# A fused attention and two feed-forward layers: maxima of a block of v moved to a later unit, and eight stores of decoded weights spread over twenty units

## Chip, cores and metric

One core of one Trainium2 chip. The metric is the device time of one execution in microseconds (us), the median of several runs. Before the change three runs gave a median of 1037.03 us (1035.72 to 1040.48).

## What is computed

```python
def _attn_ref(q, k, v, tau):                      # q, k, v: 1 x 6016 x 256
    qn = q / (np.linalg.norm(q, axis=1, keepdims=True) + 1e-06)
    kn = k / (np.linalg.norm(k, axis=1, keepdims=True) + 1e-06)
    s = kn.transpose(0, 2, 1) @ qn / tau          # 256 x 256
    a = softmax of s over its last axis
    return v @ a
def _moe_ref(x, w_in, w_out):                     # 256 -> 2048 -> 256
    h = x @ w_in
    return (h * np.cos(h)) @ w_out
def _moe2_ref(x, w_in, w_out):                    # 256 -> 2048 -> 256
    h = x @ w_in
    return (h / (1.0 + np.exp(-h))) @ w_out
reference = moe2(moe(attn(q, k, v, tau)))
```

The weights arrive as 64-bit words and are decoded to float32 on the chip. Each matrix is held as a high and a low part, so that a product is three matmul passes (high-high, low-high, high-low).

## The kernel before

The 6016 tokens are cut into eleven blocks of 512 and one of 384 (`BLOCKS`, numbered 0 to 11). First the scores are summed over all tokens, and the softmax is folded into the first layer's weights `wa`. Then the first layer with its cosine runs over the blocks, and after it the second layer with its sigmoid. The change lies in the loop of the first layer (from L997).

A *unit* `(b, m)` is one block times one eighth of the 2048 hidden columns (m = 0 to 7). Sixteen units alternate between blocks 0 and 1 (`TURNS = 16`, loop index `i` below 16), then units follow block by block: i = 16 is (2, 0), i = 24 is (3, 0), and so on to block 11. There is no scheduler: `tc.manual_schedule()` takes the instructions of each engine in the order in which the loop emits them, and each engine and each DMA queue works its own list in that order. Unit i emits, in this order:

- on TensorE (PE) the products `h` (`emit_h`, L715, 12 matmuls); for the first unit of the next block, the `bound` (below) is also emitted in unit m = 7;
- on ScalarE (ACT) the cosine of `h` (`emit_first`, L726) and then the high part `hi` of the unit before (`emit_split`, L746); on VectorE (DVE) the low part `lo` of the unit before (L747), then the product with the cosine, `t` (`emit_cos`, L739);
- the eight stores of `wa` and `wo1` (L1027 to L1029, 1 MB each, two in each of the units i = 16 to 19) into the DRAM tiles `kept`, which only a fallback for large arguments (`general`) reads;
- from block 3 on, in units m = 0 and m = 5, one step of decoding the second layer's weights: ACT takes the absolute value (L315), POOL rounds the low word (L290), DVE clamps, shifts and joins the sign (L296, L297, L303), POOL adds the low word (L306) and builds the forms (L351, L353, L354), and the SyncE queue (SP) stores them (L967, L972) and loads the next raw 0.5 MB (L270);
- in unit m = 2 the load of the next block of v, `vraw` (L389, 0.5 MB, one buffer);
- in unit m = 3 the split of `vraw` on GpSimd (POOL: `xhi` L435, `xlo` L442), and `span_of`, the maxima over groups of 128 tokens of the absolute values of `vraw`, on DVE (L395);
- on PE the second product `o` of unit i - 2 (`emit_o1`, L757, 12 matmuls), which needs that unit's `hi` and `lo`;
- one step of preparing the previous block for the second layer (`emit_x2`): from m = 2 on `forms_first` (L767, DVE), `forms_second` (L772 and L773, DVE), the high parts (L778, ACT), the low parts (L786, DVE, in m = 5 and m = 6), and then the stores of `xs` (L831, SP).

`bound` (L419 to L429) multiplies the block's maxima by the weights' maxima (L423, PE) and keeps on DVE whether the cosine's argument is small (`small`, L427 to L429). It is emitted in unit m = 7 of the block before, and from block 2 on the cosine takes it as a factor. The first call of `span_of`, for block 2, stands in unit i = 14 (L1046).

Of the kernel before, what the change touches and what calls it, by code (L numbers as in the profile page):

```python
# [9 lines left out]
F32 = mybir.dt.float32  # L10
# [21 lines left out]
NB = len(BLOCKS)  # L32
# [34 lines left out]
TURNS = 16  # L67
# [153 lines left out]
def direct(ctx, tc, qk, vT, tau, w_in1, w_out1, w_in2, w_out2, outT, dp, kept, within):  # L221
    nc = tc.nc
# [14 lines left out]
    wa = [wp.tile(QUAD, F32R, tag="quad", name=f"wa{i}", bufs=8) for i in range(4)]  # L237
    wo1 = [wp.tile(QUAD, F32R, tag="quad", name=f"wo1_{i}", bufs=8) for i in range(4)]
# [117 lines left out]
    def w_in(w, name, to=None, size=PIECE, **kw):  # L356
        n = size // CH
        src = w.rearrange("(a p) f -> p a f", p=P)
        cut = [slice(j * n, (j + 1) * n) for j in range(DFF // n)]
        to = None if to is None else [to[:, :, c] for c in cut]  # L360
        return Weights(name, [src[:, :, c] for c in cut], to=to, size=size, **kw)

    def w_out(w, name, size=PIECE, **kw):
        n = size // C
        src = w.rearrange("(f p) e -> p f e", p=P)
        return Weights(name, [src[:, n * j : n * (j + 1), :] for j in range(NF // n)], size=size, **kw)
# [7 lines left out]
    def halves(t):  # L374
        return t.rearrange("p s (h b) -> p s h b", h=2)

    def turns(t):
        return t.rearrange("p s (b h) -> p s h b", h=2)
# [3 lines left out]
    def x_tile(s, b):  # L382
        t = xp.tile([P, NU, HB], F32R, tag=f"x{s}", name=f"x{s}{b}")
        return t.rearrange("p s c -> p (s c)")[:, : CH * TB].rearrange("p (a n) -> p a n", a=CH)
# [7 lines left out]
    def span_of(b, raw):  # L392
        t0, n = BLOCKS[b]
        m = most[b] = wp.tile([P, CH, TB // P], BF16, tag="most", name=f"most{b}", bufs=2)
        nc.vector.tensor_reduce(  # L395
            out=m[:, :, : n // P],
            in_=raw[:, :, :n].rearrange("p a (j n) -> p a j n", n=P),
            axis=AX.X,
            op=ALU.max,
            apply_absolute_value=True,  # L400
        )
# [29 lines left out]
    def split_v(b, raw, pool=False):  # L431
        n = BLOCKS[b][1]
        hi, lo = xparts[1, b] = [x_tile(s, b) for s in ("hi", "lo")]
        if pool:
            nc.gpsimd.tensor_scalar(  # L435
                out=halves(hi[:, :, :n]), in0=turns(raw[:, :, :n]), scalar1=1.0, scalar2=1.0, op0=ALU.mult, op1=ALU.mult
            )
        else:
            nc.scalar.activation(halves(hi[:, :, :n]), turns(raw[:, :, :n]), AF.Copy)

        def low():
            (nc.gpsimd if pool else nc.vector).tensor_tensor(  # L442
                out=halves(lo[:, :, :n]), in0=turns(raw[:, :, :n]), in1=halves(hi[:, :, :n]).bitcast(F32), op=ALU.subtract
            )

        return low
# [57 lines left out]
    def steps_of(names):  # L504
        for name in names.split():
            calls[name]()
# [36 lines left out]
    for g, n in enumerate(GROUPS):  # L543
# [22 lines left out]
        if g in FINE:  # L566
            k = len(fine)
# [46 lines left out]
    for a in range(CH):  # L614
        nc.vector.scalar_tensor_tensor(
            out=E[:, a], in0=S[a], scalar=r[:, 1, a : a + 1], in1=rq, op0=ALU.mult, op1=ALU.mult
# [88 lines left out]
    def h_room(u):  # L705
        return next_room().tile([P, 2, TB], F32, tag="h", name=f"h{u[0]}_{u[1]}")

    def emit_h(u, hp):
        b, m = u
        n = BLOCKS[b][1]  # L710
        x = xparts[1, b]
        for s in range(2):
            todo = [(wa_at(i, a, 2 * m + s), columns(x[k][:, a, :n])) for i, k in PASSES for a in range(CH)]
            for i, (lhsT, rhs) in enumerate(todo):
                nc.tensor.matmul(hp[:, s, :n], lhsT, rhs, start=(i == 0), stop=(i == len(todo) - 1))  # L715
# [245 lines left out]
    def sink(name):  # L961
        def forms(m, t):
            if (name, m) in HELD:
                to = hp_.tile([P, 2, NS, P], F32R, tag="stage", name=f"stage_{name}{m}")
                weight_forms(w2[name][m], to[:, :, NU], t)
                first[name, m] = dp.tile([P, 2, P], F32, name=f"{name}_first{m}")
                nc.sync.dma_start(out=first[name, m], in_=to[:, :, NU].bitcast(F32))  # L967
            else:
                to = hp_.tile([P, 2, NS, P], F32R, tag="stage", name=f"stage_{name}{m}")
                weight_forms(to[:, :, :NU], to[:, :, NU], t)  # L970
                later[name, m] = dp.tile([P, 2, NS, P], F32, name=f"{name}_dram{m}")
                nc.sync.dma_start(out=later[name, m], in_=to.bitcast(F32))  # L972

        return forms
# [11 lines left out]
    def fetch_third():  # L986
        key = third.pop(0)
        fetch(key, as_forms(wp.tile(QUAD, F32R, tag="quad", name=f"{key[0]}_{key[1]}", bufs=8)))
# [8 lines left out]
    for i, u in enumerate(units):  # L997
        b, m = u
        steps_of(EARLY["ahead"].get(i, ""))
        if i == TURNS - 1:  # L1000
            pro.close()
            hp_ = ctx.enter_context(tc.tile_pool(name="held", bufs=1))
            for name, k in HELD:
                w2[name][k] = hp_.tile([P, 2, NU, P], F32R, name=f"{name}_{k}")
            y_room = ExitStack()
            yp = y_room.enter_context(tc.tile_pool(name="yp", bufs=1))
            WI2 = w_in(w_in2, "wi2", forms=sink("wi2"))
            WO2 = w_out(w_out2, "wo2", forms=sink("wo2"))
        hp = h_room(u) if m or b < 2 else opened
        emit_h(u, hp)  # L1010
        halved = i + 1 < len(units) and units[i + 1][0] > 1 and units[i + 1][1] == 0
        if halved:
            emit_o1(units[i - LAG], parts[i - LAG], (0,))
            opened = h_room(units[i + 1])
            bound(units[i + 1][0], opened[:, 0])
        t = emit_first(u, hp)
        steps_of(EARLY["amid"].get(i, ""))
        if pend is not None:
            parts[pend[0]] = emit_split(units[pend[0]], pend[1])
        steps_of(EARLY["inner"].get(i, ""))  # L1020
        emit_cos(u, hp, t)
        pend = (i, t)
        if i + 5 in range(TURNS, TURNS + 4):
            span_of_weights(i + 5 - TURNS)
        if i == TURNS - 2:
            spread_weights()
        if TURNS <= i < TURNS + 4:  # L1027
            for ts, ds in zip((wa, wo1), kept):
                nc.sync.dma_start(out=ds[i - TURNS], in_=ts[i - TURNS].bitcast(F32))  # L1029
        if i == len(units) - 1:  # L1030
            nc.vector.tensor_copy(within, every[0:1])
        steps_of(EARLY["outer"].get(i, ""))
        if i == TURNS - 1:
            WI2.load(2)
        if i >= TURNS + NPAIR and m in (0, 5):
            W = WI2 if WI2.decoded < NPAIR else WO2
            if W.decoded < NPAIR:
                W.decode()
                W.load()
        if (b, m) in ((6, 2), (6, 7)):  # L1040
            WO2.load()
        if i == TURNS - 4:
            vraw = load_v(2)
        if i == TURNS - 2:
            split_v(2, vraw)()
            span_of(2, vraw)  # L1046
        if i > TURNS and m == 2:
            if b < NB - 1:
                vraw = load_v(b + 1)
            else:  # L1050
                p1_room.close()
                sp = ctx.enter_context(tc.tile_pool(name="sp", bufs=2, side="right"))
                qp = sp
                load_x2(0)
                for key in SECOND:
                    fetch(key, sp.tile([P, 2, NS, P], F32R, name=f"{key[0]}_{key[1]}", bufs=1))
        if i > TURNS and m == 3 and b < NB - 1:
            split_v(b + 1, vraw, pool=True)()
            span_of(b + 1, vraw)
        if b == NB - 1 and m % 2 == 1:  # L1060
            fetch_third()
        if (b, m) == (NB - 1, 4):
            fetch(STAGED, hp_.tile([P, 2, NS, P], F32R, tag="stage", name="wo2_4"))
        if i >= LAG:
            v = units[i - LAG]
            emit_o1(v, parts.pop(i - LAG), (1,) if halved else (0, 1))
            if v[1] == NPAIR - 1:
                steps += [lambda b=v[0]: steps.__setitem__(slice(0, 0), emit_x2(b))] if steps else emit_x2(v[0])
            elif steps:
                steps.pop(0)()  # L1070
                if i in DOUBLED:
                    steps.pop(0)()
            if v[0] == NB - 1 and v[1] % 2 == 1:
                fetch_third()
# [23 lines left out]
    for j in range(len(units) + LAG2):  # L1098
# [6 lines left out]
        if p is not None:  # L1105
            k = (j - 1) % 2
# [131 lines left out]
```

## Time and profile before

| | |
|---|---|
| median of three runs | 1037.03 us |
| the profiled execution | 1035.96 us, its span 1034.2 us |
| mean granted TensorE clock | 0.991 of full |
| PE, DVE, ACT, POOL busy | 97%, 80%, 65%, 31% |
| DMA | 120.94 MB, 117 GB/s over the span |
| first layer's blocks 2 to 11 | from about 146 to 590 us |

The profiled execution's time is the span plus what lies outside the first and the last instruction. A row of a timeline gives the start in us, the duration in us, engine, line, operation, output <- input with shapes, the count, and in brackets how long the engine stood idle before it and who ended that.

### The profile page before, as it was taken

To read this page: it belongs to the slowest core of one execution; us is meant where nothing else is said; L and a number is where in the kernel's file an instruction comes from. 1 tells how busy PE (TensorE), PEld (TensorE's weight loads), DVE (VectorE), ACT (ScalarE), POOL (GpSimd) and SP (SyncE) were. 2 spreads that over 40 slices of the span, in tenths; PEclk is the share of its full clock that TensorE was granted. 3 is DMA by queue.
4 is the path that set the end of the run, shared out by engine and by line. 5 is a ranking of instruction groups with operands and counts; after the bars stand their busy time and mean duration, and the time that the engine had idled before them with its cause. 6 is when DMAs were issued, how large, how long until landed. Compare 5 with 4: busy or idle time off the path is not lost.

```text
span 1034.2 us, 16562 instructions
## 1 busy us (share of the span) xinstructions
PE 1004.7 (97%) x6484; PEld 925.3 (89%) x6484; DVE 829.5 (80%) x1067; ACT 676.2 (65%) x1075; POOL 321.0 (31%) x295
## 2 busy tenths in 40 slices
PE   8999999999899999989999999999999999999998
PEld 7768878888778788877889999999999999999997
DVE  5799887686867678586776789999999989999972
ACT  6786665555445445544554688888878888888863
POOL 3433320345655474565543011111111111111100
PEclk9999999999999999999999999999999999999999
DMA  9946121115052331605225961220220220220101
GB/s 338 363 155 252 42 102 72 72 47 178 25 188 106 109 133 46 214 30 185 103 85 227 415 261 55 89 82 23 83 93 12 82 93 12 83 93 24 50 22 39
DMA packets 31415, 120.94 MB, mean 117 GB/s; under 512 B 2786, under 2 KB 4706, under 8 KB 27106
## 3 DMA queue, kind: packets, MB, share of 16 engines
q1 hardware_dynamic: 31186, 119.61, 31.2%
q8 instruction: 53, 0.87, 0.3%
q14 instruction: 32, 0.26, 0.1%
q10 hardware_dynamic: 144, 0.20, 0.1%
HBM read 70.25 MB, written 49.55 MB: 116 GB/s over the span
## 4 chain that ended last, share of the span: by engine, by line
PE 80%; DVE 7%; DMA 6%; issue 3%; ACT 3%; POOL 1%; SPq 0%; DVEq 0%; ACTq 0%; POOLq 0%
PE o L860 20%; PE o L757 17%; PE h L715 17%; PE xz L860 11%; PE ys L860 9%; DMA vraw<-vT_dram 4%; DVE lo L747 2%; PE o L902 2%; DMA qk<-qk_dram 1%; PE S L534 1%; DVE t L739 1%; DVE most L395 1%; PE pw L659 1%; ACT t L726 1%; PE xz L891 1%
## 5 line engine op out<-in xcount | busy, mean ns | idle before, releaser
L726 ACT ACTIVATE t<-h,half_pi,small 128x1024 f32<-128x1024 f32 (+1 forms) x80 | 95.1, 1188 | 216.0 <-PE h L715 171.5
L747 DVE TENSOR_TENSOR lo<-t,hi 128x1024 fp32r<-128x1024 f32 (+1 forms) x96 | 145.6, 1516 | 96.4 <-ACT hi L746 96.3
L786 DVE TENSOR_TENSOR lo<-t,hi 128x768 fp32r<-128x768 f32 (+1 forms) x176 | 194.5, 1115 | 27.8 <-ACT hi L778 27.6
L860 PE MATMUL o<-hi,wo 128*128 128x256 f32 x1232 | 215.5, 275 | 0.0
L715 PE MATMUL h<-xhi,wa 128*128 128x512 f32 (+1 forms) x768 | 197.4, 379 | 1.3 <-DVE t L739 1.3
L757 PE MATMUL o<-hi,wo 128*128 128x512 f32 (+1 forms) x768 | 197.3, 380 | 0.0
L860 PEld LDWEIGHTS o<-hi,wo 128*128 128x128 f32 x1232 | 187.5, 192 | 0.0
L778 ACT ACTIVATE hi<-t 128x768 fp32r<-128x768 f32 (+1 forms) x175 | 167.9, 959 | 27.7 <-PE o L860 27.0
L773 POOL TENSOR_TENSOR t<-t 128x256 f32<-128x256 f32 x88 | 64.5, 732 | 378.9 <-DVE t L772 304.2
L860 PE MATMUL o<-lo,wo 128*128 128x256 f32 x616 | 169.4, 275 | 0.0
L715 PEld LDWEIGHTS h<-xhi,wa 128*128 128x128 f32 x768 | 145.1, 191 | 24.3 <-issue 3.8
L757 PEld LDWEIGHTS o<-hi,wo 128*128 128x128 f32 x768 | 144.6, 191 | 19.0
L757 PE MATMUL o<-lo,wo 128*128 128x512 f32 (+1 forms) x384 | 116.2, 385 | 15.9 <-DVE lo L747 15.9
L860 PE MATMUL xz<-x2hi,wi 128*128 128x256 f32 x704 | 131.7, 275 | 0.0
L860 PEld LDWEIGHTS o<-lo,wo 128*128 128x128 f32 x616 | 118.3, 192 | 0.0
L739 DVE TENSOR_TENSOR t<-h,t 128x1024 f32<-128x1024 f32 (+1 forms) x96 | 114.5, 1193 | 0.5
L715 PE MATMUL h<-xlo,wa 128*128 128x512 f32 (+1 forms) x384 | 113.3, 377 | 0.0
L860 PEld LDWEIGHTS xz<-x2hi,wi 128*128 128x128 f32 x704 | 107.0, 192 | 0.1
L860 PE MATMUL ys<-x2hi,wi 128*128 128x256 f32 x528 | 102.3, 275 | 0.3
L746 ACT ACTIVATE hi<-t 128x1024 fp32r<-128x1024 f32 (+1 forms) x96 | 98.5, 1026 | 3.6 <-DVE t L739 3.6
L757 PEld LDWEIGHTS o<-lo,wo 128*128 128x128 f32 x384 | 73.2, 194 | 28.6 <-DVE lo L747 19.2
L860 PE MATMUL xz<-x2lo,wi 128*128 128x256 f32 x352 | 96.8, 275 | 0.0
(167 smaller groups left out, 1625.2 us busy)
## 6 DMA issues: line engine op xcount, KB each, us to landing
qk<-qk_dram SPq DMA_DIRECT2D x22, 512.0 KB, 7.7
xshi<-yhi SPq DMA_DIRECT2D x11, 896.0 KB, 7.5
xslo<-ylo SPq DMA_DIRECT2D x11, 896.0 KB, 8.5
x2hi<-xshi SPq DMA_DIRECT2D x11, 896.0 KB, 5.1
x2lo<-xslo SPq DMA_DIRECT2D x11, 896.0 KB, 6.8
wo_dram<-stage_wo SPq DMA_DIRECT2D x7, 1024.0 KB, 5.0
wi_dram<-stage_wi SPq DMA_DIRECT2D x6, 1024.0 KB, 5.0
wi<-wi_dram SPq DMA_DIRECT2D x6, 1024.0 KB, 12.8
```

What stands on the lines that cost most here:

```text
L395: nc.vector.tensor_reduce(out=m[:, :, : n // P], in_=raw[:, :, :n].rearrange("p a (j n) -> p a j n", n=P), axis=AX.X, op=ALU.max, apply_ab ...
L715: nc.tensor.matmul(hp[:, s, :n], lhsT, rhs, start=(i == 0), stop=(i == len(todo) - 1))
L726: nc.scalar.activation(t[:, :, :n], hp[:, :, :n], AF.Sin, bias=half_pi, scale=small[b])
L739: nc.vector.tensor_tensor(out=t[:, :, :n], in0=hp[:, :, :n], in1=t[:, :, :n], op=ALU.mult)
L746: nc.scalar.activation(hi[:, :, :n], t[:, :, :n], AF.Copy)
L747: nc.vector.tensor_tensor(out=lo[:, :, :n], in0=t[:, :, :n], in1=hi[:, :, :n].bitcast(F32), op=ALU.subtract)
L757: nc.tensor.matmul(o[:, e, :n], wo1_at(i, f)[:, e * P : (e + 1) * P], columns(parts[k][:, s, :n]), start=(f == 0 and (i, k) == PASSES[0]), ...
L773: eng.tensor_tensor(out=t[:, 7, :c], in0=t[:, 3, :c], in1=t[:, 6, :c], op=ALU.subtract)
L778: nc.scalar.activation(hi[:, sl, :c], t[:, 1:][:, sl, :c], AF.Copy)
L786: nc.vector.tensor_tensor(out=lo[:, sl, :c], in0=t[:, 1:][:, sl, :c], in1=hi[:, sl, :c].bitcast(F32), op=ALU.subtract)
L860: nc.tensor.matmul(out, w[:, p, ka - 1], columns(x[r][:, kb - 1, : out.shape[-1]]), start=(start and i == 0), stop=(stop and i == 2), skip ...
L902: nc.tensor.matmul(state[2, b][e][:, 0, :n], lhsT, rhs, start=(m == 0 and i == 0), stop=(m == NPAIR - 1 and i == len(todo) - 1), skip_grou ...
```

## The change

The maxima of the next block (for blocks 3 to 11) are taken in unit m = 5 and no longer in unit m = 3. The split on POOL stays in m = 3, and the load in m = 2. The eight stores are no longer issued two at a time in units i = 16 to 19, but one in each of the units i = 20, 22, ... 34, that is (2, 4), (2, 6), (3, 0), (3, 2), (3, 4), (3, 6), (4, 0) and (4, 2), in the order wa0, wo1_0, wa1, wo1_1 and so on.

```diff
-        if TURNS <= i < TURNS + 4:
-            for ts, ds in zip((wa, wo1), kept):
-                nc.sync.dma_start(out=ds[i - TURNS], in_=ts[i - TURNS].bitcast(F32))
+        if i in range(TURNS + 4, TURNS + 20, 2):
+            k = (i - TURNS - 4) // 2
+            nc.sync.dma_start(out=kept[k % 2][k // 2], in_=(wa, wo1)[k % 2][k // 2].bitcast(F32))
...
         if i > TURNS and m == 3 and b < NB - 1:
             split_v(b + 1, vraw, pool=True)()
+        if i > TURNS and m == 5 and b < NB - 1:
             span_of(b + 1, vraw)
```

## Rows read from the trace of the kernel before

**Rows 1.** The page: busy time by engine, and the chain that ended last.
```profile
PE 1004.7 (97%) x6484; PEld 925.3 (89%) x6484; DVE 829.5 (80%) x1067; ACT 676.2 (65%) x1075; POOL 321.0 (31%) x295
...
PE o L860 20%; PE o L757 17%; PE h L715 17%; PE xz L860 11%; PE ys L860 9%; DMA vraw<-vT_dram 4%; DVE lo L747 2%; PE o L902 2%; DMA qk<-qk_dram 1%; PE S L534 1%; DVE t L739 1%; DVE most L395 1%; PE pw L659 1%; ACT t L726 1%; PE xz L891 1%
```

**Rows 2.** Waits of PE: total us, times, longest.
```profile
PE o L757 <- DVE lo L747: 15.9, 7, 3.3
```

**Rows 3.** Windows: length, busy PE, PEld, DVE, ACT, POOL (count), PEclk, DMA share, GB/s.
```profile
146.20:187.80 41.60, 41.60 (x196) 36.26 (x196) 30.08 (x31) 22.94 (x25) 5.76 (x3) 1.00 0.34 130
187.80:230.90 43.10, 41.86 (x196) 36.17 (x196) 31.90 (x32) 21.50 (x23) 18.07 (x17) 1.00 0.14 50
230.90:277.40 46.50, 43.24 (x196) 37.15 (x196) 33.45 (x32) 21.38 (x23) 25.87 (x24) 0.96 0.29 99
...
187.80:546.30 358.50, 342.56 (x1554) 294.84 (x1554) 262.15 (x249) 170.76 (x177) 190.92 (x171) 0.98 0.30 107
...
264.30:267.80 3.50, 2.88 (x7) 2.32 (x8) 2.36 (x3) 2.84 (x4) 0.00 (x0) 0.51 0.00 0
```

**Rows 4.** The chain that ended last, blocks 3 and 4: start us, us, what.
```profile
208.74 4.70 DMA vraw<-vT_dram
...
252.03 6.73 DMA vraw<-vT_dram
...
264.92 3.38 PE o L757 x8
```

**Rows 5.** Timeline of DVE in units (4,3) and (4,4).
```profile
253.80 1.22 DVE L739 TENSOR_TENSOR t<-h,t 128x1024 f32<-128x1024 f32 x1
258.78 1.22 DVE L395 TENSOR_REDUCE most<-vraw 128x8 bf16<-128x1024 f32 x1 [3.76 <-DMA vraw<-vT_dram]
259.92 0.83 DVE L772 TENSOR_TENSOR y<-y 128x256 f32<-128x256 f32 x1
260.78 2.51 DVE L773 TENSOR_TENSOR y<-y 128x256 f32<-128x256 f32 x1
263.22 1.65 DVE L747 TENSOR_TENSOR lo<-t,hi 128x1024 fp32r<-128x1024 f32 x1
```

**Rows 6.** Timeline of ACT, POOL and PE in the same stretch.
```profile
256.76 1.04 ACT L746 ACTIVATE hi<-t 128x1024 fp32r<-128x1024 f32 x1
258.90 1.57 POOL L435 TENSOR_SCALAR xhi<-vraw 128x1024 fp32r<-128x1024 f32 x1 [7.83 <-DMA vraw<-vT_dram]
260.56 2.46 POOL L442 TENSOR_TENSOR xlo<-vraw,xhi 128x1024 fp32r<-128x1024 f32 x1
...
264.92 1.22 PE L757 MATMUL o<-lo,wo 128*128 128x512 f32 x2 [3.26 <-DVE lo L747]
```

**Rows 7.** Timeline of POOL and DVE in block 2.
```profile
152.06 2.42 POOL L442 TENSOR_TENSOR xlo<-vraw,xhi 128x1024 fp32r<-128x1024 f32 x1
...
152.43 3.14 DVE L747 TENSOR_TENSOR lo<-t,hi 128x1024 fp32r<-128x1024 f32 x1 [2.06 <-ACT hi L746]
...
165.51 0.43 DVE L773 TENSOR_TENSOR y<-y 128x256 f32<-128x256 f32 x1
```

**Rows 8.** Timeline of DVE and POOL in units (3,5) and (3,6).
```profile
222.02 1.23 DVE L747 TENSOR_TENSOR lo<-t,hi 128x1024 fp32r<-128x1024 f32 x1 [1.14 <-ACT hi L746]
...
225.96 0.94 DVE L786 TENSOR_TENSOR ylo<-y,yhi 128x768 fp32r<-128x768 f32 x1
226.82 2.31 DVE L747 TENSOR_TENSOR lo<-t,hi 128x1024 fp32r<-128x1024 f32 x1
...
226.19 1.87 POOL L306 TENSOR_TENSOR wv_wi<-wv_wi,raw_wi 128x512 int32<-128x512 int32 x1 [7.51 <-DVE wv_wi L303]
```

**Rows 9.** The SP queue: the first and the last of eight stores, and L972.
```profile
74.45 0.47 SPq L1029 DMA_DIRECT2D wa_kept<-wa  x1
...
147.05 0.37 SPq L1029 DMA_DIRECT2D wo_kept<-wo  x1
...
251.10 0.32 SPq L972 DMA_DIRECT2D wi_dram<-stage_wi  x1
```

## Prediction

> **What bounds the kernel now.** I read the busy shares first, then what TensorE (PE) waits for, then the stretches between the bounds of successive blocks, then the chain around one of PE's waits. PE is busy 97% of the span, and matmuls make most of the chain that ended last [rows 1]; so the change can only win time in which PE stands still or runs slowly. In the list of PE's waits one line dominates: the second product of the first layer (L757) waiting for VectorE's (DVE's) `lo` of L747, 15.9 us in seven waits, 3.3 us the longest [rows 2].
>
> The windows from one `bound` to the next show where that is [rows 3]. Block 2 needs 41.60 us for 196 matmuls and PE is busy in all of it. That is my ideal for a block of 512 tokens, 0.212 us a matmul. Blocks 3 to 10 together take 358.50 us (the row 187.80:546.30) where 8 x 41.60 = 332.8 would do: **25.7 us are lost.** PE's busy time there is 342.56, so 15.9 us are idle. The other 9.8 us lie inside busy time. [...] Where PE's idle time in a block is short, 43.10 - 41.86 = 1.24 us, the clock stays at 1.00 [rows 3].
>
> The chain tells who holds `lo` [rows 4, 5, 6]. In unit (4,3) `vraw` is issued at 252.03 and needs 6.73 us to land. DVE has done its `t` of that unit by 255.02, and the next instruction in its queue is the maxima of L395, which wait 3.76 us for the landing and run at 258.78. Behind them stand L772 and L773, two small subtractions that now coincide with GpSimd's (POOL's) split of the same `vraw` (L435 at 258.90, L442 at 260.56): 0.83 and 2.51 us. Only then, at 263.22, does `lo` start, although ScalarE (ACT) had its `hi` ready at 256.76 + 1.04 = 257.80. PE was free for it at 264.92 - 3.26 = 261.66. So without the maxima `lo` has 261.66 - 257.80 - 1.23 = **2.6 us of slack** (1.23 is its undisturbed length, [rows 8]), and with them it comes 3.3 us late.
>
> **The change part by part.** *The maxima leave unit 3.* The nine reductions of L395 for blocks 3 to 11 go from m == 3 to m == 5 of the block before: two units later, three after the load. In unit 3 this removes the 3.76 us wait and the 1.14 us from the maxima's start to the next start. L772 and L773 then run from 255.02, about 3.9 us before POOL starts on `vraw`, as in block 2, where L773 took 0.43 us [rows 7]; so the pair is done by 256, before `hi`. What is late next in unit 4 is nothing: `lo` starts at 257.80 and ends at 259.0, while POOL's L435 starts at 258.90. The bound of what this part gives is all of the 25.7 us.
>
> *POOL's split may now hold `lo` instead of L773.* In block 2 a `lo` that started 0.37 us after POOL's L442 took 3.14 us and ended 1.09 us after L442 did [rows 7]; held by one L442 it thus ends at most 2.46 + 1.09 = 3.55 us after its start, against 3.86 available (261.66 - 257.80). So one hold costs PE nothing, and block 2 lost nothing by it. [...] Being held by two in a row is a rival below.
>
> *The maxima join unit 5.* There DVE has `lo`, `t`, three steps of the decode and L786: in block 3 from 222.02 to 226.90, 4.88 us [rows 8], of a unit of 41.60 / 8 = 5.20. With 1.14 more it is 6.02, so the next `lo` begins some 0.8 us late. L786 now starts behind POOL's L306, which took 1.87 us beside it [rows 8]: bounds 0 and 1.87, I take 0.7, because the reduction runs beside most of L306. The `lo` after it was held 2.31 - 1.23 = 1.1 us by L306 already; bounds 0 and 1.1, I take 0.5, since L306 will be over by then. The sum, 0.8 + 0.7 + 0.5 = 2.0 us, stays under the 2.6 of slack; the upper end, 3.8, would cost 1.2 per block. Queued behind the maxima on DVE are only L786 (for the store of `xs`, which nobody reads before the second layer) and that `lo`; decode's L303, for which POOL waits, stands ahead of them. The bound itself reads the maxima in unit 7, some 8 us later. If DVE were full in unit 6 too, the lateness would carry on; it has `lo`, `t` and one more L786 there, an estimated 1.14 + 1.14 + 1.3 = 3.6 us of 5.2 (by the lengths of `lo` and L786 in rows 8), and catches up.
>
> *Does the wait for `vraw` only move?* `vraw` lands 6.73 us after 252.03, at 258.76. In unit 5 the maxima come two units, 10.4 us, after 255.02, and three decode steps later still: 267. 8 us remain.
>
> *The eight stores.* They are issued now from 74.45 to 147.05 [rows 9], on both sides of the load of `vraw` for block 3, and no engine waits for them. So taking them away there gives nothing (bounds 0 and 0: PE is busy in every us from 146.2 to 187.8). They cost the SyncE (SP) queue about 0.4 us each to issue. In the new place, units 20, 22, ... 34, they depend on tiles that are long complete, so none blocks SP; but the one of unit (3,2) and the one of (4,2) stand directly ahead of the loads of `vraw` for blocks 4 and 5. What 1 MB ahead costs: the load at 208.74, which has at most half a MB right ahead, lands in 4.70 us, the one at 252.03, with the 1 MB store of L972 at 251.10 ahead as well, in 6.73 [rows 4, 9]. The difference is 2.0 us, plus 0.4 to issue; bounds 0 and 4.7 (a whole load's time), I take 2.4. The maxima have 8 us, so DVE doesn't wait. But POOL's split of block 5 moves to about 261.2, its L442 then runs from 262.8 to 265.3 and meets the `lo` of unit 5 (start 257.80 + 5.20 = 263.0), which ends at 265.3 + 1.09 = 266.4, 2.2 us late. With 0.8 and 0.5 more behind the maxima, `lo` of unit 6 is 3.5 us late, 0.9 over its slack. I charge 1.0 us for block 4 and 0.3 for block 3 (bounds 0 and 4 for both together). The other six stores pass only transfers that are wanted tens of us later: raw weights for the next decode, `xs`, the staged weights. POOL's queue has no instruction moved.
>
> **Sum.** 25.7 - 1.0 - 0.3 - 0.2 (the later `lo` of the other six blocks, between 0 and 6 x 1.2) = 24.2 us. The profiled execution took 1035.96 us (span 1034.2): 1011.8. The median of the three runs lies 1.07 above it, 1037.03, so I forecast the median at **1012.5**, between 1011.8 and 1012.8. The second layer and the front have no step of the change and I carry them over.
>
> **Rivals.** (a) *Unit 5 overflows.* DVE's 6.02 us in 5.20 and a long hold make PE wait 1 us in each of eight blocks, too short for the clock to fall: 1035.96 - 25.7 + 8 = 1018. For: the `lo` behind unit 5 was held 2.31 us by L306 already [rows 8]. Against: 2.6 us of slack. Chance 0.10.
> (b) *POOL holds `lo` through both its instructions* in unit 4: L435 and L442 in a row from 258.90 end at 263.02 [rows 6], `lo` 1.09 later, 264.1 against 261.66: 2.4 us, the idle time of the present, and at that length the drops of 1.7 in perhaps half the blocks: 8 x 3.3 = 26, no change, 1036. For: L773 started just after L442 and was held to its end. Against: `lo` starts 1.1 us before L435 in this block. In blocks where `vraw` lands early it starts later; if half are hit, 1023. Chance 0.07, of which 0.03 without change.
> (c) *Slower.* The lateness of unit 5 snowballs: L435, L442 and L306 each hold one DVE operation in turn, 1.57 + 2.46 + 1.87 = 5.9 us [rows 6, 8], with the 0.8 of the overfull unit 6.7, less 2.6 of slack 4.1, and 1.7 for the clock: 5.8 in each block, 8 x 5.8 = 46, 1035.96 - 25.7 + 46 = 1056. It decides from 25.7 / 8 = 3.2 us per block upward. Against: between unit 4 and L306 DVE idles over 1 us waiting for `hi` [rows 8], which takes up one hold. Chance 0.04.
> (d) *The stores delay `vraw` beyond unit 5*, so the wait only moves. It can be so in two blocks of eight: 2 x 5 = 10, 1022. Chance 0.04.
>
> **How the numbers follow.** The forecast has 0.75, from 1009.5 (all 25.7 and a run like the fastest) to 1017. The range reaches to (a), (d) and the half of (b): **1009.5 to 1022**, which leaves out about 0.1. About 0.5%, 5.2 us, is what a measurement of this kernel can tell from no change. Faster by more: 0.75 + 0.10 + 0.04 + 0.04 = 0.93; within: 0.03; slower: 0.04.
>
> **What would show it.** PE's wait for L747 shrinks from 15.9 us to under 3, the granted clock is 1.00 in all nine windows, each near 41.6 to 42 us; L395 has no wait for `vraw`; L773 falls from 2.5 to 0.43; `vraw` for blocks 4 and 5 lands some 2.4 us later. I am wrong if PE waits for the `lo` of unit 5 or 6 in most blocks, or for a `lo` that ends 1.09 us after L442.

## Result and the profile after

The changed kernel takes 1013.17 us (median of four runs, 1012.83 to 1014.98), against 1038.4 for the kernel before in the same set. The ratio is 0.976, 95% interval 0.973 to 0.979: 2.4% faster. The forecast was 1012.5 us, range 1009.5 to 1022. The profiled execution took 1013.34 us with a span of 1011.5, so the span fell by 22.7 us from 1034.2.

The page of the changed kernel, busy time and the chain that ended last, to be set beside [rows 1]:

```profile
PE 997.9 (99%) x6484; PEld 921.9 (91%) x6484; DVE 804.2 (80%) x1067; ACT 677.0 (67%) x1075; POOL 327.9 (32%) x295
...
PE o L757 22%; PE h L715 22%; PE o L860 20%; PE xz L860 12%; PE ys L860 9%; DMA qk<-qk_dram 2%; PE o L902 2%; PE S L534 1%; PE pw L659 1%; DVE t L739 1%; PE xz L891 1%; PE ys L891 1%; DVE lo L747 1%; DVE acc L582 0%; DVE largest L405 0%
```

The load of `vraw`, 4% of the chain before, is gone from it. The waits of PE in the changed kernel (total us, times, longest), beside [rows 2]:

```profile
PE h L423 <- DVE most L395: 2.0, 1, 2.0
...
PE o L757 <- DVE lo L747: 0.6, 1, 0.6
PE h L423 <- DVE t L739: 0.4, 1, 0.4
```

The 15.9 us in seven waits for `lo` have become 0.6 in one. The windows of the changed kernel from one `bound` to the next (columns as in [rows 3]) show blocks 2, 3, 4, 5, 6, then 7 to 10 together, and last the 3.5 us behind the first bound:

```profile
145.74:189.02 43.28, 43.28 (x196) 37.44 (x196) 28.81 (x31) 22.80 (x25) 4.76 (x3) 0.96 0.32 125
189.02:230.61 41.59, 41.59 (x195) 36.25 (x196) 28.08 (x32) 21.44 (x23) 19.06 (x17) 1.00 0.34 127
230.61:273.73 43.12, 42.06 (x196) 36.18 (x196) 31.81 (x32) 21.38 (x23) 25.54 (x22) 1.00 0.48 180
273.73:315.45 41.72, 41.72 (x195) 36.16 (x196) 30.27 (x32) 21.56 (x23) 26.40 (x23) 1.00 0.37 133
315.45:357.04 41.59, 41.59 (x196) 36.25 (x196) 29.06 (x32) 21.45 (x23) 26.34 (x23) 1.00 0.37 133
357.04:523.41 166.37, 166.37 (x778) 145.02 (x778) 117.75 (x125) 85.77 (x89) 102.81 (x89) 1.00 0.35 124
146.20:149.70 3.50, 3.50 (x10) 2.79 (x9) 3.42 (x4) 2.12 (x3) 0.26 (x1) 0.51 0.48 150
```

Blocks 3 to 10 now take 41.59 + 43.12 + 41.72 + 41.59 + 166.37 = 334.4 us instead of 358.5 [rows 3]: 24.1 us gained where 24.2 were forecast. Only block 4 is clearly off the ideal, by 1.5 us. Block 2 *lost* 1.7 us: behind the same 2.0 us wait of the first bound that the kernel before had, the clock fell to 0.51 this time. That is why the span fell by only 22.7. No step of the change decides it, as the runs below show: the clock also falls there with the stores in their old place, and stays up in two profiles with the stores in their new place.

### The profile page after: what moved, and what is told of

It reads as the page before. It is cut to its first block, busy times and chain, and to the rows that moved or that the text cites. A ratio compares the mean times of both kernels' runs of the same rounds, so it can differ in the third digit from the quotient of the medians.

```text
span 1011.5 us, 16558 instructions
## 1 busy us (share of the span) xinstructions
PE 997.9 (99%) x6484; PEld 921.9 (91%) x6484; DVE 804.2 (80%) x1067; ACT 677.0 (67%) x1075; POOL 327.9 (32%) x295
## 4 chain that ended last, share of the span: by engine, by line
PE 91%; DVE 4%; ACT 2%; DMA 2%; issue 1%; POOL 0%; SPq 0%; ACTq 0%; DVEq 0%
PE o L757 22%; PE h L715 22%; PE o L860 20%; PE xz L860 12%; PE ys L860 9%; DMA qk<-qk_dram 2%; PE o L902 2%; PE S L534 1%; PE pw L659 1%; DVE t L739 1%; PE xz L891 1%; PE ys L891 1%; DVE lo L747 1%; DVE acc L582 0%; DVE largest L405 0%
## 5 line engine op out<-in xcount | busy, mean ns | idle before, releaser
L747 DVE TENSOR_TENSOR lo<-t,hi 128x1024 fp32r<-128x1024 f32 (+1 forms) x96 | 136.2, 1419 | 124.1 <-ACT hi L746 124.1
L786 DVE TENSOR_TENSOR lo<-t,hi 128x768 fp32r<-128x768 f32 (+1 forms) x176 | 194.7, 1116 | 27.0 <-ACT hi L778 26.9
L757 PE MATMUL o<-hi,wo 128*128 128x512 f32 (+1 forms) x768 | 194.8, 376 | 0.0
L773 POOL TENSOR_TENSOR t<-t 128x256 f32<-128x256 f32 x88 | 64.5, 733 | 380.5 <-DVE t L772 292.0
L715 PEld LDWEIGHTS h<-xhi,wa 128*128 128x128 f32 x768 | 144.1, 190 | 24.2 <-issue 4.2
L757 PE MATMUL o<-lo,wo 128*128 128x512 f32 (+1 forms) x384 | 113.1, 376 | 0.6 <-DVE lo L747 0.6
```

The costliest lines, as they stand in the source:

```text
L747: nc.vector.tensor_tensor(out=lo[:, :, :n], in0=t[:, :, :n], in1=hi[:, :, :n].bitcast(F32), op=ALU.subtract)
L757: nc.tensor.matmul(o[:, e, :n], wo1_at(i, f)[:, e * P : (e + 1) * P], columns(parts[k][:, s, :n]), start=(f == 0 and (i, k) == PASSES[0]), ...
L773: eng.tensor_tensor(out=t[:, 7, :c], in0=t[:, 3, :c], in1=t[:, 6, :c], op=ALU.subtract)
L786: nc.vector.tensor_tensor(out=lo[:, sl, :c], in0=t[:, 1:][:, sl, :c], in1=hi[:, sl, :c].bitcast(F32), op=ALU.subtract)
```

## Experiments

The runs came in three sets, each on one chip. Ratios are to the kernel before, timed in the same set. Each set has a median of its own for the kernel before (1035.81, 1034.18 and 1034.52 us), so kernels of different sets are compared by ratio only.

### One half of the change each

The maxima alone (stores as before):

```diff
         if i > TURNS and m == 3 and b < NB - 1:
             split_v(b + 1, vraw, pool=True)()
+        if i > TURNS and m == 5 and b < NB - 1:
             span_of(b + 1, vraw)
```

> Only the maxima move to unit 5; the eight stores stay in units i = 16 to 19. Theory (VectorE's queue stood behind the maxima's wait for vraw; the stores only cost what they delay): all of the gain and the loss of block 4 gone, about 1.5 us under the changed kernel, 1011.7 us; PE waits for lo under 0.3 us in all, every window of blocks 3 to 10 41.6 us. Rival (the stores' old place held something up and their move gave part of the gain): 2 us or more above the changed kernel, 1015 or more. Whether the clock falls behind the first bound at 146 us, as it did in the changed kernel and not before, is open: if the stores' absence there causes it, it does not fall here and another 1.7 us are gained.

Measured: 1009.59 us, ratio 0.975 (0.973 to 0.977). Windows of its trace, block 2 and then blocks 3 to 10:

```profile
144.64:186.23 41.59, 41.59 (x195) 36.25 (x196) 30.28 (x31) 22.82 (x25) 5.77 (x3) 1.00 0.34 130
186.23:519.00 332.77, 332.77 (x1554) 290.06 (x1554) 233.41 (x249) 171.78 (x177) 201.44 (x172) 1.00 0.33 115
```

All eight blocks are at the ideal, 332.8 us, with PE never idle. The maxima's move carries the whole 25.7 us. The clock did not fall behind the first bound in this profile.

The stores alone (the new loop of the stores, which puts them into the fifteen units i = 20 to 34, not into twenty as the title has it; the maxima left in m == 3):

> Only the stores move; the maxima stay in unit 3. Theory: the stores of units (3,2) and (4,2) delay vraw by some 2 us, and the maxima, with everything behind them on VectorE, wait that much longer in blocks 3 and 4; block 3's longer idle time also lets the clock fall: 2 x 2.0 + 1.7 = 5.7 us slower than the kernel before, about 1043 us. Rival (the stores' move gives part of the gain): 2 us or more faster than the kernel before.

Measured: 1042.26 us, ratio 1.006 (1.004 to 1.008), slower by 0.6%, about as much as expected. In the chain of its trace `vraw` for blocks 4 and 5, which is loaded during blocks 3 and 4, takes this long to land:

```profile
207.32 7.11 DMA vraw<-vT_dram
...
254.83 8.15 DMA vraw<-vT_dram
```

and PE's idle time ahead of the `lo` in blocks 3 and 4, then in block 5, is:

```profile
220.58 0.70 PE L757 MATMUL o<-lo,wo 128*128 128x512 f32 x2 [3.95 <-DVE lo L747]
...
268.95 0.70 PE L757 MATMUL o<-lo,wo 128*128 128x512 f32 x2 [4.82 <-DVE lo L747]
...
315.11 0.70 PE L757 MATMUL o<-lo,wo 128*128 128x512 f32 x2 [2.61 <-DVE lo L747]
```

Before, the two loads took 4.70 and 6.73 us [rows 4], and PE idled 1.24 and 3.26 us [rows 3, 6]. So 1 MB directly ahead cost these loads 2.4 and 1.4 us, and a store that nobody waits for becomes 2.7 and 1.6 us of PE time (3.95 - 1.24, 4.82 - 3.26) as long as the maxima stand in unit 3. Behind block 3's longer wait the clock now falls as well (0.96 over that block, 1.00 before; four matmuls of `h` took 1.91 us behind it, 1.03 in the next unit). Blocks 3 to 10 take 364.1 us in its trace, 358.5 before; nothing in it speaks for a gain by the stores' move.

### Where block 4's 1.5 us come from

In the changed kernel, units (4,3) to (4,6) on DVE, with POOL's split and SP's issue (timelines; some rows left out):

```profile
252.44 1.07 SPq L389 DMA_DIRECT2D vraw<-vT_dram  x1
...
255.15 0.42 DVE L773 TENSOR_TENSOR y<-y 128x256 f32<-128x256 f32 x1
257.60 1.22 DVE L747 TENSOR_TENSOR lo<-t,hi 128x1024 fp32r<-128x1024 f32 x1 [2.03 <-ACT hi L746]
...
262.78 3.12 DVE L747 TENSOR_TENSOR lo<-t,hi 128x1024 fp32r<-128x1024 f32 x1 [2.82 <-ACT hi L746]
...
268.57 1.24 DVE L395 TENSOR_REDUCE most<-vraw 128x8 bf16<-128x1024 f32 x1
269.70 1.26 DVE L786 TENSOR_TENSOR ylo<-y,yhi 128x768 fp32r<-128x768 f32 x1
270.88 1.47 DVE L747 TENSOR_TENSOR lo<-t,hi 128x1024 fp32r<-128x1024 f32 x1
...
260.77 1.54 POOL L435 TENSOR_SCALAR xhi<-vraw 128x1024 fp32r<-128x1024 f32 x1 [10.23 <-DMA vraw<-vT_dram]
262.39 2.43 POOL L442 TENSOR_TENSOR xlo<-vraw,xhi 128x1024 fp32r<-128x1024 f32 x1
```

L773 is back to 0.42 us (2.51 before, [rows 5]) and `lo` of unit 4 starts the moment `hi` is there. But the store of unit (4,2) puts POOL's split so late that L442 begins 0.39 us before the `lo` of unit 5, which is held to L442's end plus 1.08 us. Unit 5 with the maxima in it can't make that up, and the next `lo` ends 0.6 us after PE needs it. The `t` behind that `lo` is late too, and `bound` waits for it:

```profile
273.54 0.19 PE L423 MATMUL h<-most,widest 128*128 128x4 bf16 x2 [0.43 <-DVE t L739]
```

The two waits are 1.06 of the 1.5 us; the other 0.47 lie inside PE's busy time (42.06 against 41.59). Two runs take away one cause each. The stores out of the way of the loads:

```diff
+KEEP = (20, 21, 22, 23, 27, 28, 29, 30)
...
-        if i in range(TURNS + 4, TURNS + 20, 2):
-            k = (i - TURNS - 4) // 2
+        if i in KEEP:
+            k = KEEP.index(i)
```

> The changed kernel with the eight stores in units i = 20 to 23 and 27 to 30, none ahead of a load of vraw in its unit. Theory (block 4's loss of 1.5 us comes from the store ahead of its load, by way of POOL's split meeting lo): block 4 falls from 43.1 to 41.6 us, about 1011.7 us. Rival (it comes from the overfull unit 5 alone): block 4 stays at 43.1.

And the maxima in unit 4 (`m == 5` becomes `m == 4`), the stores as in the change:

> The changed kernel with the maxima in unit 4, where VectorE has no decode, and the stores as in the changed kernel. Theory (2.6 us of slack per lo): vraw has landed before unit 4's maxima in the undisturbed blocks, so no wait there; in block 4 they wait under 1 us, which the 2.8 us of idle time in that unit covers, and the lo of unit 6 is no longer late: block 4 about 41.7 us, the whole 1011.7 us. Rival (the maxima must stay two units away, or the wait returns): PE waits for lo in most blocks, 1018 us or more.

Measured: 1010.55 us, 0.975 (0.973 to 0.977), and 1009.68 us, 0.974 (0.972 to 0.976). Block 4's window in the first and in the second:

```profile
230.20:271.80 41.60, 41.60 (x198) 36.26 (x195) 29.05 (x32) 21.46 (x23) 26.33 (x23) 1.00 0.38 136
```

```profile
228.50:270.85 42.35, 41.92 (x196) 36.27 (x196) 32.58 (x31) 21.57 (x23) 25.45 (x25) 1.00 0.49 183
```

Without the store ahead of the load block 4 is at the ideal, so the store is needed for the loss; the rival that unit 5 does it alone falls. With the maxima in unit 4 half of the loss stays (42.35), where 41.7 was expected. Its timeline shows the wait for `vraw` back, but taken up by the idle time before `hi`:

```profile
258.89 1.22 DVE L395 TENSOR_REDUCE most<-vraw 128x8 bf16<-128x1024 f32 x1 [1.10 <-DMA vraw<-vT_dram]
260.62 1.23 DVE L747 TENSOR_TENSOR lo<-t,hi 128x1024 fp32r<-128x1024 f32 x1 [0.51 <-ACT hi L746]
...
260.65 3.48 POOL L442 TENSOR_TENSOR xlo<-vraw,xhi 128x1024 fp32r<-128x1024 f32 x1
```

`lo` began 0.03 us before L442, and here it was POOL's instruction that took longer: 3.48 us, against 2.43 in the changed kernel. The maxima ran at their 1.22 us beside L435. What is left of the loss comes later:

```profile
262.90 1.51 DVE L296 TENSOR_SCALAR wv_wi<-wv_wi 128x512 f32<-128x512 f32 x1
...
267.14 2.32 DVE L747 TENSOR_TENSOR lo<-t,hi 128x1024 fp32r<-128x1024 f32 x1
...
270.65 0.19 PE L423 MATMUL h<-most,widest 128*128 128x4 bf16 x2 [0.43 <-DVE t L739]
```

The first decode step takes 1.51 us beside the late L442 (0.41 in the changed kernel), the `lo` of unit 6 takes 2.32 beside POOL's L306, and again it is `bound` that waits for the `t` behind it, not `o` for `lo`. So the late split alone, with unit 5 relieved of the maxima, still costs 0.75 us; this reading of its path rests on the timeline, no run takes the path away.

### The wait or the place?

The kernel before with its maxima in unit 3, but `vraw` loaded in unit m = 0, ahead of the decode:

```diff
+        if i >= TURNS + NPAIR and m == 0 and b < NB - 1:
+            vraw = load_v(b + 1)
         if i >= TURNS + NPAIR and m in (0, 5):
...
-                vraw = load_v(b + 1)
+                if b == 2:
+                    vraw = load_v(b + 1)
```

> The kernel before, with the load of vraw issued in unit m = 0 ahead of the decode (block 2 as before); maxima in unit 3 and stores as before. Theory (the loss is the wait of the maxima for a load that stands behind the staged weights' store on the SyncE queue, not the place of the maxima): no wait for vraw on VectorE, POOL's split runs at once after the decode, PE's wait for lo under 1 us, about as fast as the changed kernel, 0.973 to 0.978 of the kernel before. Rival (1.1 us more work for VectorE in unit 3 is itself what makes lo late): PE waits for lo in most blocks, 0.99 or more.

Measured: 1010.49 us, 0.974 (0.970 to 0.979). SP issues the load at 237.90 in block 4 instead of 252.03 [rows 4], DVE never waits for it, and PE never waits for `lo` (some rows of block 4, then the window of blocks 3 to 10):

```profile
237.90 1.33 SPq L389 DMA_DIRECT2D vraw<-vT_dram  x1
...
252.10 3.23 DVE L747 TENSOR_TENSOR lo<-t,hi 128x1024 fp32r<-128x1024 f32 x1
...
256.39 1.20 DVE L395 TENSOR_REDUCE most<-vraw 128x8 bf16<-128x1024 f32 x1
...
188.75:521.49 332.74, 332.74 (x1554) 290.65 (x1554) 258.90 (x249) 171.42 (x177) 198.66 (x171) 1.00 0.33 115
```

The same gain with the maxima left where they were: the loss lay in the wait, and the place of the maxima only mattered because everything on DVE stood behind that wait. The run does not separate the wait itself (3.76 us) from what it led to, L773 starting beside POOL's split and taking 2.51 us instead of 0.43 [rows 5, 7]: the early load takes away both.

### How much room unit 5 has

The changed kernel, the unchanged one repeated on the same chip, with the maxima taken twice or three times in unit 5 (more work than the reference asks for; three times has one line more, and in both the tile of the maxima has four buffers instead of two):

```diff
         if i > TURNS and m == 5 and b < NB - 1:
             span_of(b + 1, vraw)
+            span_of(b + 1, vraw)
```

> The changed kernel unaltered, on the chip of the following runs, so that they can be set beside it. 0.976 of the kernel before, as measured, if nothing depends on the chip. The clock's fall behind the first bound at 146 us: if it is chance it is absent in some of its profiles and of those of its kin; if the stores cause it, it is there again.

> The changed kernel with the maxima of each block taken twice in unit 5 (the second into another tile; nine reductions more, 1.14 us each). Theory (2.6 us of slack, of which the late lo behind unit 5 uses about 1.3): 2.4 us late is still within it, so only block 4, which is at its limit, pays 1.1 us and perhaps the clock's 1.7: 1 to 3 us above the changed kernel. Rival (no slack is left): 1.1 us in each of eight blocks, 9 us or more.

> The same with the maxima taken three times. Theory: 3.6 us late, 1.0 over the slack in each of eight blocks and 2.3 in block 4, so about 9 to 12 us above the changed kernel, with PE waiting for lo in all blocks from 3 to 10. Rival (the slack is larger than worked out): less than 4 us above it.

Measured: 1013.37 us unaltered (0.977, 0.972 to 0.982); its profile shows the clock's fall behind the first bound again. One run each of 1020.82 and 1034.65 us for the other two, 7.4 and 21.3 above. Both theories were off. Taken twice, PE does not wait for `lo` outside block 4, so that much of the account held, and the clock falls once more, behind block 4, as the theory had allowed (four matmuls of `h` take 1.70 us there, 1.03 a little later), after waits of 1.36 and 0.43 us; rival (a) had put 1 us as too short for that. But a typical block costs 42.19 us, 0.6 more, and the wait is another:

```profile
319.37 0.19 PE L426 MATMUL h<-most,widest 128*128 128x4 bf16 x2 [0.39 <-DVE t L742]
...
319.57:361.76 42.19, 41.81 (x195) 36.20 (x196) 31.41 (x33) 21.51 (x23) 26.24 (x22) 1.00 0.37 131
```

(Lines are shifted by 3 there: L426 is `bound`, L742 is `t`.) The kernel has two rooms in PSUM (where its code puts PE's products) for `h`, used in turn. `bound` of unit 7 writes into the one that held unit 6's `h`, and so needs that unit's `t`, which reads it and stands behind the late `lo`. The wait is 0.39 of the 0.6 us. Taken three times, a typical block costs 44.38 us, 2.8 more, of which 1.2 is the wait for `lo` that I had expected:

```profile
322.57 0.70 PE L760 MATMUL o<-lo,wo 128*128 128x512 f32 x2 [1.23 <-DVE lo L750]
323.70 0.19 PE L426 MATMUL h<-most,widest 128*128 128x4 bf16 x2 [0.43 <-DVE t L742]
...
325.78 1.10 PE L718 MATMUL h<-xhi,wa 128*128 128x512 f32 x4 [0.48 <-POOL stage_wi L353]
...
323.89:368.27 44.38, 42.25 (x196) 36.25 (x196) 31.99 (x34) 21.52 (x23) 26.44 (x23) 1.00 0.35 124
```

A third wait, 0.48 us of the next block's first `h`, was in no theory. The profile names POOL's L353 as what ended it, whose tile that `h` does not read; it does need DVE to have read `bound`'s result out of the same room. Its cause stays open.

So unit 5 of the changed kernel stands close to its limit. In block 5, DVE and PE:

```profile
312.19 1.48 DVE L747 TENSOR_TENSOR lo<-t,hi 128x1024 fp32r<-128x1024 f32 x1
313.59 1.21 DVE L739 TENSOR_TENSOR t<-h,t 128x1024 f32<-128x1024 f32 x1
...
315.25 0.20 PE L423 MATMUL h<-most,widest 128*128 128x4 bf16 x2
```

`t` ends at 314.80 and `bound` runs at 315.25, with PE busy up to it: 0.45 us are left, not the 1.3 that `lo` alone suggests.

### A version that beats both

Four kernels on one chip: the changed one, the maxima alone, and two that also shorten the first bound's wait. The third has the maxima in unit 4, the stores as before, and block 2's split on POOL; the fourth in addition loads block 2 in unit i = 8 and takes its maxima in i = 9. The fourth's edit in the front, of which the third has the split's line alone:

```diff
-        if i == TURNS - 4:
+        if i == TURNS - 8:
             vraw = load_v(2)
+        if i == TURNS - 7:
+            span_of(2, vraw)
         if i == TURNS - 2:
-            split_v(2, vraw)()
-            span_of(2, vraw)
+            split_v(2, vraw, pool=True)()
```

> The changed kernel unaltered, beside the three that follow on one chip: 0.974 to 0.978 of the kernel before.

> Only the maxima moved, again, now on the same chip as the changed kernel. Theory: the stores' new places cost what block 4 showed, 1.5 us, so this one is 1 to 3 us faster than the changed kernel. Rival: no difference, the two were on different chips.

> Maxima in unit 4, stores as in the kernel before, and block 2's split on POOL instead of ScalarE and VectorE. Theory: VectorE's queue behind which the first bound waits loses 1.2 us, so that wait falls from 2.0 to 0.9 us, and the clock no longer falls behind it: 1 to 3 us faster than the variant with the maxima moved alone. Rival: POOL holds VectorE's two-input operations there and gives it back: no difference.

> As the one before, with block 2's load of v one place earlier and its maxima taken in unit i = 9, where VectorE idled 2.4 us. Theory: the first bound's wait goes altogether, another 1 us: 2 to 4 us faster than the variant with the maxima moved alone. Rival: VectorE is late in units 9 to 14 in any case, and the wait stays near 1 us.

Measured: 1011.36 us (1010.43 to 1012.33), 1011.39 (1010.89 to 1011.99), 1010.05 (1008.59 to 1011.43) and 1008.69 (1008.02 to 1009.19); ratios 0.976 (0.972 to 0.980), 0.976 (0.973 to 0.980), 0.975 (0.971 to 0.980) and 0.974 (0.970 to 0.978). On one chip the maxima alone are no faster in time than the whole change, so that expectation missed; the 1.5 us of block 4 are seen in the traces, while the times scatter by as much, and with them the mean clock (0.997 to 1.000). The third failed: its first bound still waited 2.0 us, and its runs overlap with those of the maxima alone. A `lo` of DVE in unit i = 13 ran beside POOL's split and took 2.52 us (1.22 in the second profile of the maxima alone), and the 1.2 us were given back:

```profile
133.37 1.51 POOL L435 TENSOR_SCALAR xhi<-vraw 128x1024 fp32r<-128x1024 f32 x1
...
133.44 2.52 DVE L747 TENSOR_TENSOR lo<-t,hi 128x1024 fp32r<-128x1024 f32 x1
...
144.44 0.20 PE L423 MATMUL h<-most,widest 128*128 128x4 bf16 x2 [1.98 <-DVE most L395]
```

In the fourth the wait is 0.79 us, not gone altogether as the theory had it, but its runs lie clear of those of the changed kernel and of the maxima alone: 2.7 us less by the medians, about 26 us under the kernel before. It is not shown to beat the early load or the whole change with the maxima in unit 4, which have the same ratio of 0.974 on other chips.

## Why the prediction was right

- *The maxima leave unit 3*, 25.7 us: right. The run with the maxima alone has all eight blocks at the ideal, and the early load gives as much without moving them. In the changed kernel DVE has no wait for `vraw` in any of these blocks. The 9.8 us inside PE's busy time came back together with the 15.9 of idle time: the granted clock over blocks 3 to 10 was 0.98 before [rows 3] and is 1.00 with the maxima alone. Before, it was 0.51 in the 3.5 us behind block 4's wait [rows 3], where eight matmuls took 3.38 us [rows 4] instead of 8 x 0.212 = 1.70.
- *POOL's split may hold `lo`*: right, in block 4 it did (3.12 us), and the `o` that needs that `lo` did not wait; the next one did, after unit 5 had added its lateness. In both orders seen here the instruction that began second took longer: `lo` 3.12 us, begun 0.39 us behind L442 (1.23 undisturbed, [rows 8]), and with the maxima in unit 4 L442 3.48 us, begun 0.03 us behind `lo` (2.43 in the changed kernel).
- *The maxima join unit 5*: `lo` of unit 6 was 1.1 us late at its start in block 5 (312.19 against `hi` at 311.12) and 1.3 at its end, where I summed 2.0; no wait. The reduction took 1.21 us there beside L306, which took 1.30. The step was sound for `lo`, but "queued behind the maxima on DVE are only L786 and that `lo`" left out the `t` behind them. The tightest consumer is `bound`, by way of that `t` and its PSUM room, with 0.45 us left in block 5. It cost nothing there because the lateness was smaller than estimated; in block 4 it cost 0.43 us. By these rows it bears an estimated 1.3 + 0.45 = 1.75 us of lateness, less than the 2.0 that I had summed; that it cost nothing in most blocks is partly luck.
- *The eight stores*: I charged 1.0 us for block 4 and 0.3 for block 3; measured 1.5 and 0. POOL's split in block 4 ran 30.16 us after the block's first `bound` instead of 28.00, so 2.2 later where I had 2.4. Right in place and in the path to `lo` (0.62 us of waiting, 0.9 forecast); the 0.43 us of `bound` were not in the sum.
- *The front is carried over*: not quite. The clock fell behind the first bound in this profile, 1.7 us, so the sign "1.00 in all nine windows" failed for block 2, and the profiled execution is 1.5 us above the 1011.8 of the sum. The median is nearer to the forecast, 0.7 us, because this time it lies just under the profiled execution and not 1.07 above it.
- Rivals (a) to (d): none came. (b)'s two holds in a row did not occur; (d) was excluded by the maxima's wait, zero in every block. The 1.7 us that (b) and (c) add for the clock were an estimate: no window of blocks 3 to 10 of the changed kernel shows them (1.00 in each), and the fall in its block 2 cost 43.28 - 41.59 = 1.7 us.

## What to carry to other kernels

In this kernel an instruction that waits for a DMA held everything behind it in its engine's queue (the maxima on DVE, 3.76 us), so its price is read from who waits for the instructions behind it; move it to where the transfer has landed, or issue the transfer ahead of whatever blocks its queue. A store that nobody waits for can still have a price if it stands directly ahead of a load that somebody does (here 2.7 and 1.6 us of PE time). When work is moved into a fuller stretch, work out the slack of every consumer behind it, the release of a PSUM room among them, not just of the one that waited before.

## What the runs showed of the hardware

Equal waits of PE did not have equal consequences for its clock. The first bound waited 2.0 us in each of these kernels but the last, with block 2 loaded early: in the profile of the changed kernel the granted clock fell to 0.51 behind it, in those of the kernel before and of the maxima alone it stayed at 1.00, and in the second profile of the maxima alone it fell. In all, thirteen of the profiles have that wait of about 2.0 us, and the clock fell behind it in eight (the first two matmuls of `o` with `lo` behind it took 1.04 to 1.06 us in these, 0.59 in the other five): in all three of the changed kernel, in the run with the stores out of the way of the loads, in the early load, in the maxima taken twice and three times, and in one of the two of the maxima alone. So the stores' new place neither suffices (the stores alone and the maxima in unit 4 have it and did not fall) nor is needed (the early load does not have it); that it has no part at all is not shown, and what decides a fall stays open. In the kernel before a wait of 2.61 us was followed by a fall (0.57 from 312 to 316 us), in the run with the stores alone one of 2.61 us was not (two matmuls of `o` at 316.51 us took 0.59 us). The fall in block 2 of the changed kernel cost 1.7 us (43.28 against 41.59), and the spread of the kernel before goes with the clock: in the last set its run at a mean clock of 0.996 took 1032.69 us, one at 0.991 took 1036.50, and one at 0.987 took 1040.77. Taking the waits away made the times not only shorter but closer together (1032.69 to 1040.77 in seven runs before, 1008.02 to 1009.19 in four of the fourth).
